# Attention ahead of two mixtures of experts: the products of a pack with v as one step, and the last 64 rows of q and k turned as whole blocks

## The chip, the cores and the metric

The kernel runs on one core of a Trainium2 chip. The metric is the device time of one execution in microseconds, lower is better. The engines are named as in the profile: PE is TensorE (PEld its weight load), DVE is VectorE, ACT is ScalarE, POOL is GpSimd, and SP is the queue that issues most transfers.

## What is computed

```python
# attention: batch 2, 8 heads, 576 rows, width 64; blocks of 64 rows
scores = q @ k.T / sqrt(64)
scores = where(row // 64 >= column // 64, scores, -1e9)
attn   = softmax(scores)                     # row maximum subtracted, 1e-9 in the sum
x      = attn @ v  ->  (1152, 512)
# layer 1: each row goes to the expert of its largest logit (8 experts, 512 -> 1024 -> 512)
x = gate * sigmoid(x @ w_output_gate)[expert] * (relu(x @ w1[expert]) @ w2[expert])
# layer 2: the same without the output gate, and with a capacity per expert
```

All data are float32. The scores and the layers are computed as three products of split halves each (a high part, a low part, and the two cross products), the products with v as plain float32.

## The kernel before, in words

The change lies in the attention, which takes the first third of the run. The two batches of a head lie side by side: tiles `qn`, `kn`, `vn` (`nat` in the code) hold 128 rows by 64 + 64 columns, in five column groups. Four are full blocks of 128 rows; the fifth holds the last 64 rows of the sequence in partitions 0 to 63. q and k are rotated over two such tiles, v over three. Partitions 64 to 127 of the fifth group of v are zeroed once at the start (L1271), since a product reads them.

`prep_steps(h)` turns q and k of a head: four whole blocks of k, then of q (L1366), and in its third step the last 64 rows of q and of k, each as a 64x64 product (L1353). Of these it makes high and low parts with ACT and DVE, and POOL adds `kf` and `qf` out of them (L1359, L1360).

A head has nine blocks of 64 query rows; they are worked off in three packs of three blocks (`packs`). For a pack there are four kinds of work:

- `qk_steps`: for each of its three blocks, the scores on PE (L1386, or L1383 for the two shortest), the row maximum on DVE (L1387), the exponentials with their sum on ACT (L1390). Each block is a step; with each comes a call of `extra_step()`, which does one step of whatever waits in the list `extra` (the preparation of the next head; at the end the routing of the first layer, `begin_first`).
- `group_steps` (`transp`): the exponentials turned in 128x128 blocks on PE (L1413), 7 blocks in two groups for the first pack, 9 blocks in three groups for the others, and copied to `tp` by ACT (L1417), the third group by DVE (L1419).
- `pv_steps` (`pv`): the products with v (L1439), by column chunk: 3, 4 or 5 chunks for the first, second, third pack, two matmuls a chunk, one per batch, each of which fills 64 of the 128 output rows. A float32 matmul shows as two records in the trace, so a chunk has four. After the last chunk come three copies to `ot` on ACT (L1442 to L1444) and four small operations on DVE (L1445 to L1450). Each chunk is a step of its own.
- the last step of `pv`: four matmul records with `mv` that bring the result into rows and give the logits (L1453, L1454), the scaling on DVE (L1457, L1459), the sum of logits (L1461, on POOL, for the last head on DVE), and then `after_pv`: the rows of `x1` to memory, the loads of v for a later head, and, for the last head's first pack, the routing is put into `extra`.

The main loop takes one step in turn of: the scores of the pack after this one, the turning of this pack, the products with v of the pack before it. Heads 6 and 7 are interleaved by packs. `extra_step` leaves out its third and fourth call once the routing has begun. After the loop the last pack's `pv_steps` are worked off with an `extra_step` each.

The order in which this text issues the instructions is not the order on the engines. In the attention a planner simulates the engines at build time with a table of costs, and gives each engine, among the instructions that are ready in that simulation, the one that the text issues first. From the first layer on, the order is that of the text.

Of the kernel before, what the change touches and what calls it, by code (L numbers as in the profile page):

```python
# [32 lines left out]
def kernel(  # L33
# [15 lines left out]
    nc = tc.nc  # L49
    V = nc.vector  # L50
    B, H, S, D = q.shape
# [3 lines left out]
    P = 128  # L55
    BLK = 64
# [30 lines left out]
    ident = const.tile([P, P], F32, name="ident")  # L87
# [653 lines left out]
    class Moe:  # L741
# [17 lines left out]
        def load(self, s, c0=0, c1=8):  # L759
            if s not in self.at:  # L760
                self.where(s)
            e, cond = self.at[s]
            load_w(self.w1, self.w2, e, c0, c1, cond=cond)
# [477 lines left out]
    with ExitStack() as actx:  # L1241
# [7 lines left out]
        def pst():  # L1249
            return ps_t.tile([P, 512], F32, tag="t", name="pst")  # L1250
# [4 lines left out]
        NC4 = S // P  # L1255
        REM = S - NC4 * P
        NR = {"q": 2, "k": 2, "v": 3}
        nat = {nm: [ap1.tile([P, NC4 + 1, 2 * D], F32, name=f"{nm}n{i}") for i in range(n)] for nm, n in NR.items()}
# [7 lines left out]
        for i in range(2):  # L1266
            for b in range(0, NB, 2):
                if i == 0:
                    nc.gpsimd.memset(pbuf[i][b][:, (b + 1) * BLK :], 0.0)
        for t_ in nat["v"]:  # L1270
            nc.gpsimd.memset(t_[REM:P, NC4, :], 0.0)  # L1271


# [46 lines left out]
        def prep_steps(h):  # L1320

            i = h % 2
            kh = ap2.tile([P, S], F32R, tag="kh", name=f"kh{h}")
            kl = ap2.tile([P, S], F32R, tag="kl", name=f"kl{h}")
            st[h] = dict(qh=qhb[i], ql=qlb[i], kh=kh, kl=kl, p=pbuf[i],
                         mx=ap2.tile([P, NB], F32, tag="mx", name=f"mx{h}", bufs=3),
                         sm=ap2.tile([P, NB], F32, tag="sm", name=f"sm{h}", bufs=3),
                         ri=ap2.tile([P, NB], F32, tag="ri", name=f"ri{h}", bufs=3), pt={})

            mv = st[h]["mv"] = mvs[h % 3]  # L1330
            for bb, r in enumerate(halves):
                for j in (bb, 2):
                    nc.gpsimd.tensor_copy(mv[r, j, D:W], wgs[r, h, :])

            def qout(ps, b0, b1):
                src = [ps[r, :].rearrange("p (b j) -> p b j", j=BLK) for r in halves]
                for r, x in zip(halves, src):
                    if h == 0 and r is halves[1]:
                        V.tensor_scalar(qhb[i][r, b0:b1, r], x, SCALE, None, op0=ALU.mult)
                    else:  # L1340
                        nc.scalar.activation(qhb[i][r, b0:b1, r], x, AF.Copy, scale=SCALE)
                for r, x in zip(halves, src):
                    V.scalar_tensor_tensor(out=qlb[i][r, b0:b1, r], in0=x, scalar=SCALE, in1=qhb[i][r, b0:b1, r].bitcast(F32), op0=ALU.mult, op1=ALU.subtract)

            def kout(ps, a, z):
                nc.scalar.copy(kh[:, a:z], ps)
                V.tensor_tensor(kl[:, a:z], ps, kh[:, a:z].bitcast(F32), op=ALU.subtract)

            for nm in ("k", "q", "r"):
                ps = pst()  # L1350
                if nm == "r":
                    for j, x in enumerate(("q", "k")):
                        nc.tensor.transpose(ps[:, j * BLK : j * BLK + REM], nat[x][h % NR[x]][0:REM, NC4, :], ident[0:REM, 0:REM])  # L1353
                    qout(ps[:, 0:BLK], NB - 1, NB)
                    kout(ps[:, BLK : 2 * BLK], NC4 * P, S)
                    if 2:
                        qf = st[h]["qf"] = ap2.tile([P, 2, P], F32, tag="qf", name=f"qf{h}")
                        kf = st[h]["kf"] = ap2.tile([P, 2 * BLK], F32, tag="kf", name=f"kf{h}")
                        nc.gpsimd.tensor_tensor(kf, kh[:, 0 : 2 * BLK].bitcast(F32), kl[:, 0 : 2 * BLK].bitcast(F32), op=ALU.add)  # L1359
                        anchors["qf", h] = nc.gpsimd.tensor_tensor(qf, qhb[i][:, 0:2, :].bitcast(F32), qlb[i][:, 0:2, :].bitcast(F32), op=ALU.add).ins  # L1360
                    ready.add(h)
                    if h + NR["q"] < H:
                        load(h + NR["q"], "kq")
                else:
                    for c in range(NC4):
                        nc.tensor.transpose(ps[:, c * P : (c + 1) * P], nat[nm][h % NR[nm]][:, c, :], ident)  # L1366
                    if nm == "q":
                        qout(ps, 0, NB - 1)
                    else:
                        kout(ps, 0, NC4 * P)  # L1370
                yield
# [53 lines left out]
        def pv(h, pk):  # L1425

            s = st[h]
            t0 = POS[packs[pk][0][0]]
            po = pst()
            hc = slice(h * D, (h + 1) * D)  # L1430
            ts_ = slice(t0, t0 + 3)
            lo, hi = slice(0, BLK), slice(BLK, P)
            nc_ = max(c for p_, c in s["pt"] if p_ == pk) + 1
            for c in range(nc_):
                w = s["pt"][pk, c]
                n = w.shape[1]
                for bb in range(B):
                    r = slice(bb * D, (bb + 1) * D)
                    nc.tensor.matmul(po[r, 0 : n * BLK], nat["v"][h % NR["v"]][:, c, r], w[:, :, r], start=(c == 0), stop=(c == nc_ - 1))  # L1439
                if c == nc_ - 1:  # L1440
                    ot = OT.next()
                    nc.scalar.copy(ot[:, 0 : 2 * BLK], po[:, 0 : 2 * BLK])  # L1442
                    nc.scalar.copy(ot[lo, P + lo.start : P + lo.stop], po[lo, 2 * BLK : 3 * BLK])
                    anchors["ot", h, pk] = nc.scalar.copy(ot[hi, P + hi.start : P + hi.stop], po[hi, 2 * BLK : 3 * BLK]).ins  # L1444
                    V.tensor_scalar_add(s["sm"][:, ts_], s["sm"][:, ts_], 1e-9)  # L1445

                    ri, sm_ = s["ri"], s["sm"]
                    V.reciprocal(ri[:, ts_], sm_[:, ts_])
                    V.reciprocal(ri[hi, t0 : t0 + 1], sm_[lo, t0 + 1 : t0 + 2])
                    V.reciprocal(ri[lo, t0 + 1 : t0 + 2], sm_[hi, t0 : t0 + 1])  # L1450
                yield
            ps = po[:, 3 * BLK : 512]
            nc.tensor.matmul(ps[:, 0 : 2 * W], ot[:, 0:P], s["mv"][:, 0:2, :], start=True, stop=True)  # L1453
            last[0] = nc.tensor.matmul(ps[:, 2 * W : 3 * W], ot[:, P : 2 * P], s["mv"][:, 2, :], start=True, stop=True).ins  # L1454
            p3 = ps[:, 0 : 3 * W].rearrange("p (t w) -> p t w", w=W)
            rb = ri[:, ts_].unsqueeze(2)
            V.tensor_tensor(x1[:, ts_, hc], p3[:, :, 0:D], rb.to_broadcast([P, 3, D]), op=ALU.mult)  # L1457
            lg = lg1[:, ts_, :] if h == 0 else ap2.tile([P, 3, 2 * E], F32, tag="lg", name=f"lg_{h}_{pk}")
            V.tensor_tensor(lg, p3[:, :, D:W], rb.to_broadcast([P, 3, 2 * E]), op=ALU.mult)  # L1459
            if h > 0:  # L1460
                (V if h == H - 1 else nc.gpsimd).tensor_tensor(lg1[:, ts_, :], lg1[:, ts_, :], lg, op=ALU.add)  # L1461
# [83 lines left out]
        for _ in prep_steps(0):  # L1545
            pass
# [6 lines left out]
        for i, (h, pk) in enumerate(stages):  # L1553
            if (h, pk) == (2, 0):
                with tc.issue_after(anchors["qf", 1]):
                    for f in later:
                        f()
                    nc.gpsimd.tensor_copy(capf, capi[:, 0:1])
                    nc.sync.dma_start(x1d[N : N + 1, :], zrow[0:1, :])
                    nc.sync.dma_start(x2d[N : N + 1, :], zrow[0:1, :])  # L1560
            if pk == 0 and h + 1 < H and h + 1 not in st:
                extra.append(prep_steps(h + 1))
            qs_ = iter(())
            tail = False
            if i + 1 < len(stages):
                while stages[i + 1][0] not in ready and extra:
                    extra_step()
                qs_ = qk_steps(*stages[i + 1], tail)
            live = [(qs_, group_steps(h, pk), before)[i_] for i_ in (0, 1, 2)]
            while live:  # L1570
                for it in list(live):
                    try:
                        next(it)
                    except StopIteration:
                        live.remove(it)
            before = pv_steps(h, pk)
# [234 lines left out]
```

## Time and profile before

| what | value |
|---|---|
| median of 3 runs | 416.88 us (416.2 to 418.99) |
| the profiled execution, its device time | 416.57 us |
| its span, first to last instruction | 414.8 us |
| PE busy in the span | 386.4 us (93%) |
| DVE | 289.4 us (70%) |
| ACT | 254.1 us (61%) |
| POOL | 101.6 us (25%) |
| granted TensorE clock, mean | 0.976 |

The busy time of PE is an upper bound of its work: matmuls overlap, and their ends are modelled, so that a stretch can show PE busy all the time though it runs below its pace. The pace is read better from the starts of the matmuls. The attention lies in the first 139 us, the two layers behind it.

### The profile page before, as it was taken

Reading aid. Unit: us, or ns where it says so; the run is one execution under the profiler, and the core shown is the slowest. Engines: PE = TensorE matmul, PEld = TensorE weight load, DVE = VectorE, ACT = ScalarE, POOL = GpSimd, SP = SyncE. Lnnn points to the kernel's source line nnn. Section 1 sums busy time; section 2 is a strip of 40 time slices with the busy share of each in tenths; the row PEclk is TensorE's granted clock in tenths of the full one; section 3 lists DMA queues with packets and bytes.
Section 4 is the critical chain, followed back from the end, with each engine's and each line's share of the span. In section 5 each row is a group of like instructions: output and inputs, shape, how many; then the busy total and the mean of one; then the engine's idle time right before and its main releaser. Section 6 shows DMA issues by size and latency. Waiting matters only on the chain. (4 is left out here: it accounts for less than half of the span.)

```text
span 414.8 us, 7835 instructions
## 1 busy us (share of the span) xinstructions
PE 386.4 (93%) x2443; PEld 295.3 (71%) x2443; DVE 289.4 (70%) x755; ACT 254.1 (61%) x531; POOL 101.6 (25%) x211
## 2 busy tenths in 40 slices
PE   4899999999996899999999999978999999999992
PEld 3677887887775678888888866656777888856540
DVE  4577667766788697798988944679789999911010
ACT  2678778878775552877878611553679998821110
POOL 8452201212100204103212110121710287200100
PEclk9999999999997999999999999978899999999998
DMA  6649932510106802991661388360795999899890
GB/s 139 114 105 285 294 103 61 144 24 7 57 22 223 297 3 84 305 345 54 216 242 52 122 335 321 137 228 2 248 384 188 333 371 401 288 384 390 297 362 29
DMA packets 65111, 82.88 MB, mean 200 GB/s; under 512 B 34368, under 2 KB 38976, under 8 KB 65060
## 3 DMA queue, kind: packets, MB, share of 16 engines
q1 hardware_dynamic: 62180, 72.98, 52.4%
q0 software_dynamic: 2880, 9.31, 6.1%
q8 instruction: 21, 0.34, 0.3%
q14 instruction: 30, 0.25, 0.2%
HBM read 91.57 MB, written 11.80 MB: 249 GB/s over the span
## 5 line engine op out<-in xcount | busy, mean ns | idle before, releaser
L187 DVE TENSOR_TENSOR wl<-raw,wh 128x1024 fp32r<-128x1024 f32 x52 | 61.3, 1220 | 2.3 <-ACT wh L169 2.3
L169 ACT CAST wh<-raw 128x1024 fp32r<-128x1024 f32 x52 | 51.5, 1052 | 1.0 <-DMA raw<-in_moe_w_dram 0.8
L719 PE MATMUL ph<-wh,xh 128*128 128x512 f32 x120 | 50.7, 422 | 1.4 <-ACT xh L708 1.4
L719 PE MATMUL ph<-wh,xl 128*128 128x512 f32 x120 | 48.6, 405 | 0.0
L719 PE MATMUL ph<-wl,xh 128*128 128x512 f32 x120 | 48.2, 402 | 0.0
L1387 DVE TENSOR_REDUCE mx<-s 128x1 f32<-128x256 f32 (+8 forms) x72 | 34.4, 486 | 17.5 <-PE s L1386 4.6
L1390 ACT ACTIVATE p<-s,mx 128x256 f32<-128x256 f32 (+8 forms) x72 | 37.8, 527 | 10.1 <-DVE mx L1387 9.2
L1413 PE MATMUL pst<-ident,p 128*128 128x128 f32 x200 | 39.1, 291 | 0.4 <-DVE lg L1459 0.3
L187 DVE TENSOR_TENSOR wl_a<-raw,wh_a 128x1024 fp32r<-128x1024 f32 x28 | 33.2, 1220 | 0.3 <-ACT wh_a L169 0.2
L1439 PE MATMUL pst<-tp,vn 128*64 128x128 f32 (+2 forms) x384 | 32.8, 297 | 0.1
L169 ACT CAST wh_a<-raw 128x1024 fp32r<-128x1024 f32 x28 | 28.1, 1061 | 5.8 <-DMA raw<-in_moe_w_dram 5.7
L733 PE MATMUL py<-wh_a,hh 128*128 128x512 f32 x72 | 30.1, 418 | 0.0
L1413 PEld LDWEIGHTS pst<-ident,p 128*128 128x128 f32 x200 | 25.4, 150 | 6.1 <-issue 2.4
L1417 ACT COPY tp<-pst 128x384 f32<-128x384 f32 (+1 forms) x48 | 24.5, 533 | 8.2 <-PE pst L1413 7.9
L733 PE MATMUL py<-wh_a,hl 128*128 128x512 f32 x72 | 28.7, 399 | 0.6 <-DVE hl L814 0.6
L733 PE MATMUL py<-wl_a,hh 128*128 128x512 f32 x72 | 28.8, 401 | 0.0
L187 DVE TENSOR_TENSOR wl_b<-raw,wh_b 128x1024 fp32r<-128x1024 f32 x24 | 28.4, 1220 | 0.6 <-ACT wh_b L169 0.5
L1386 PE MATMUL s<-kh,qh 128*128 128x320 f32 (+3 forms) x64 | 26.0, 406 | 2.7 <-ACT p L1390 1.4
L719 PEld LDWEIGHTS ph<-wh,xh 128*128 128x128 f32 x120 | 23.2, 193 | 6.4 <-ACT xh L708 1.9
L738 POOL DMA_INDIRECT out_dram<-ys,ig x7 | 11.9, 1705 | 63.5 <-ACT ys L921 57.1
L719 PEld LDWEIGHTS ph<-wh,xl 128*128 128x128 f32 x120 | 23.1, 192 | 6.1 <-DVE xl L709 1.3
L1439 PEld LDWEIGHTS pst<-tp,vn 128*64 128x64 f32 x384 | 21.1, 142 | 8.7 <-issue 3.8
(353 smaller groups left out, 868.9 us busy)
## 6 DMA issues: line engine op xcount, KB each, us to landing
raw<-in_moe_w_dram SPq DMA_DIRECT2D x132, 512.0 KB
rx<-in_moe_w_dram SPq DMA_DIRECT2D x20, 512.0 KB
out_dram<-zrow SPq DMA_DIRECT2D x9, 256.0 KB
x2d<-zrow SPq DMA_DIRECT2D x9, 256.0 KB
kn<-in_k_dram SPq DMA_DIRECT2D x16, 128.0 KB
qn<-in_q_dram SPq DMA_DIRECT2D x16, 128.0 KB
vn<-in_v_dram SPq DMA_DIRECT2D x16, 128.0 KB
x1d<-x SPq DMA_DIRECT2D x3, 576.0 KB
```

What stands on the lines that cost most here:

```text
L169: nc.scalar.copy(whs[i], raw[:, c, :] if src is None else src)
L187: V.tensor_tensor(wls[i], raw[:, c, :] if src is None else src, whs[i].bitcast(F32), op=ALU.subtract)
L719: yield nc.tensor.matmul(out_, l[:, c * P : (c + 1) * P], r[:, cols], start=(c == 0 and j == 0), stop=(c == KD - 1 and j == 2))
L733: nc.tensor.matmul(y, l[:, cs], r[:, rs], start=(first and j == 0), stop=(last and j == 2))
L738: nc.gpsimd.indirect_dma_start(out=dest, out_offset=bass.IndirectOffsetOnAxis(ap=io.bitcast(U32), axis=0), in_=ys, in_offset=None, bounds_ ...
L1386: nc.tensor.matmul(ps[:, a:z], s[l][:, b, :], s[r][:, a - o : z - o], start=(j == 0), stop=(j == 2))
L1387: anchors["mx", h, pk] = V.tensor_reduce(out=s["mx"][:, t : t + 1], in_=ps[:, o : o + n], op=ALU.max, axis=AX.X, negate=True).ins
L1390: anchors["p", h, pk] = nc.scalar.activation(s["p"][b][:, 0:n], ps[:, o : o + n], AF.Exp, bias=s["mx"][:, t : t + 1], accum_out=s["sm"][:, ...
L1413: last[0] = nc.tensor.transpose(ps[:, j * P : (j + 1) * P], s["p"][b][:, c * P : (c + 1) * P], ident).ins
L1417: anchors["tp", h, pk] = nc.scalar.copy(fp, ps[:, 0:n]).ins
L1439: nc.tensor.matmul(po[r, 0 : n * BLK], nat["v"][h % NR["v"]][:, c, r], w[:, :, r], start=(c == 0), stop=(c == nc_ - 1))
```

## The change

Three edits. The upper halves of the fifth column group are zeroed for q and k as well as for v. The last 64 rows of q and k are then turned as whole 128x128 blocks, over rows of which the lower half is zero; of the 128 result columns the first 64 are used as before. And the `yield` in `pv` moves out of the loop over the chunks: all products of a pack with v, the copies to `ot` and the four DVE operations are one step, and the products with `mv` with what follows them are the second and last.

```diff
-        for t_ in nat["v"]:
+        for t_ in nat["q"] + nat["k"] + nat["v"]:
             nc.gpsimd.memset(t_[REM:P, NC4, :], 0.0)
...
                     for j, x in enumerate(("q", "k")):
-                        nc.tensor.transpose(ps[:, j * BLK : j * BLK + REM], nat[x][h % NR[x]][0:REM, NC4, :], ident[0:REM, 0:REM])
+                        nc.tensor.transpose(ps[:, j * P : (j + 1) * P], nat[x][h % NR[x]][:, NC4, :], ident)
                     qout(ps[:, 0:BLK], NB - 1, NB)
-                    kout(ps[:, BLK : 2 * BLK], NC4 * P, S)
+                    kout(ps[:, P : P + BLK], NC4 * P, S)
...
                     V.reciprocal(ri[hi, t0 : t0 + 1], sm_[lo, t0 + 1 : t0 + 2])
                     V.reciprocal(ri[lo, t0 + 1 : t0 + 2], sm_[hi, t0 : t0 + 1])
-                yield
+            yield
             ps = po[:, 3 * BLK : 512]
```

With the step count of `pv_steps` the calls of `extra_step` shift at the end: the routing enters `extra` in the second round of its stage instead of the fourth, so its first step is called one stage's last round earlier, and the last pack's steps give two calls instead of six.

## Rows read from the trace of the kernel before

**Rows 1.** Windows: stretch, its length, busy us (instructions) by engine, clock, DMA.
```profile
20.00:118.00 98.00, 96.64 (x807) 77.16 (x806) 69.67 (x237) 76.66 (x257) 21.91 (x105) 1.00 0.42 116
118.00:131.00 13.00, 9.34 (x85) 7.65 (x81) 12.27 (x80) 8.97 (x29) 0.29 (x1) 0.92 0.49 173
```

**Rows 2.** Waits of PE from 20 to 118 us: total, times, longest.
```profile
PE s L1383 <- ACT p L1390: 0.9, 4, 0.3
```

**Rows 3.** Timeline of PE, products with v in three runs: start, length, instruction.
```profile
98.11 0.55 PE L1439 MATMUL pst<-tp,vn 128*64 128x192 f32 x4
98.59 0.66 PE L1413 MATMUL pst<-ident,p 128*128 128x128 f32 x4
99.18 0.44 PE L1439 MATMUL pst<-tp,vn 128*64 128x128 f32 x4
99.55 0.44 PE L1413 MATMUL pst<-ident,p 128*128 128x128 f32 x2
99.92 0.66 PE L1439 MATMUL pst<-tp,vn 128*64 128x128 f32 x8
100.50 0.33 PE L1366 MATMUL pst<-ident,kn 128*128 128x128 f32 x1
```

**Rows 4.** Timeline of PE, the same sixteen records in one run.
```profile
117.48 1.20 PE L1439 MATMUL pst<-tp,vn 128*64 128x192 f32 x16
118.61 0.38 PE L1386 MATMUL s<-kh,qh 128*128 128x256 f32 x1
```

**Rows 5.** Timeline of PE, four blocks turned with no change of shape behind.
```profile
46.51 0.60 PE L1366 MATMUL pst<-ident,qn 128*128 128x128 f32 x4
46.95 0.22 PE L1383 MATMUL s<-kf,qf 128*128 128x64 f32 x1
```

**Rows 6.** Timeline of PE, the first run of products with v.
```profile
19.81 0.55 PE L1439 MATMUL pst<-tp,vn 128*64 128x192 f32 x4
```

**Rows 7.** Timeline of PE, the last rows of q and k turned.
```profile
62.52 0.60 PE L1413 MATMUL pst<-ident,p 128*128 128x128 f32 x4
63.05 0.27 PE L1353 MATMUL pst<-ident,qn 64*128 64x64 f32 x1
63.17 0.22 PE L1353 MATMUL pst<-ident,kn 64*128 64x64 f32 x1
63.32 0.38 PE L1386 MATMUL s<-kh,qh 128*128 128x256 f32 x1
63.54 0.28 PE L1386 MATMUL s<-kl,qh 128*128 128x256 f32 x1
63.66 0.28 PE L1386 MATMUL s<-kh,ql 128*128 128x256 f32 x1
```

**Rows 8.** Timeline of POOL and PE in the first 17 us.
```profile
2.84 0.49 POOL L1271 MEMSET vn<- 64x128 f32 x3
...
6.42 0.37 PE L1353 MATMUL pst<-ident,qn 64*128 64x64 f32 x1
...
7.89 0.69 PE L1386 MATMUL s<-kh,qh 128*128 128x384 f32 x1 [1.01 <-DVE qh L1339]
...
9.90 0.46 POOL L1359 TENSOR_TENSOR kf<-kh,kl 128x128 f32<-128x128 f32 x1
...
16.48 0.38 PE L1383 MATMUL s<-kf,qf 128*128 128x128 f32 x2
```

**Rows 9.** Waits of SP's queue: total, times, longest.
```profile
SPq L1464 <- DVE lg L1459: 27.5, 4, 14.6
```

**Rows 10.** Timeline, the third group of a pack turned and copied.
```profile
114.54 0.44 PE L1413 MATMUL pst<-ident,p 128*128 128x128 f32 x2
...
115.01 0.42 DVE L1419 COPY tp<-pst 128x256 f32<-128x256 f32 x1 [0.33 <-PE pst L1413]
```

**Rows 11.** Timeline of PE and one window, the end of the attention.
```profile
130.14 0.19 PE L369 MATMUL pst<-a_rag,a_ohp 128*128 128x15 bf16 x1 [2.71 <-DVE a_ohp L347]
...
138.78 0.52 PE L706 MATMUL px<-ident,xg 128*128 128x128 f32 x3 [0.68 <-DVE lg L1459]
...
130.10:135.50 5.40, 5.36 (x39) 4.20 (x41) 3.90 (x18) 1.52 (x3) 1.29 (x2) 0.50 0.32 116
```

## The prediction

> **What bounds the kernel now.** I began with the windows, to see which engine limits the stretch that the change touches. From 20 to 118 us, the body of the attention, PE shows 96.64 us busy of 98.00, DVE 69.67 and ACT 76.66 [rows 1]: 99% against 71% and 78%. The waits of PE agree: the largest entry of that stretch is 0.9 us in four waits, for exponentials [rows 2]. So an instant taken from PE's own sequence there moves everything behind it. From 118 to 131 us the picture is another: DVE 12.27 us of 13.00, PE 9.34. There the routing of the first layer runs on DVE beside the end of the attention, and what PE saves is worth little.
>
> A busy PE isn't PE at its pace, so next I read the starts of its matmuls. Four blocks turned in a row take 46.95 - 46.51 = 0.44 us to the next start, 0.11 us a block [rows 5]. The products with v have another shape, 128x64 beside 128x128, and they come in pieces. One pack's sixteen records come in three runs: 98.11 to 100.50, 2.39 us, with six turned blocks between them (0.66 us at 0.11), which leaves 1.73 us for the products [rows 3]. The same sixteen records in one run take 118.61 - 117.48 = 1.13 us [rows 4]. Two runs more cost 0.60 us, so **each change into that shape and back costs 0.30 us**. The turning of the last rows shows the same: its shape is 64x128, and around it the spacing jumps [rows 7].
>
> **The change part by part.** *Products with v as one step.* From 19.81 us [rows 6] to the run at 117.48 [rows 4] the timeline has 39 runs. They belong to 21 packs (18 of heads 0 to 5, both first packs of heads 6 and 7, the second of head 6). With one run a pack, 18 runs go: 18 x 0.30 = 5.4 us. It can't be more by this edit, short of two packs' products standing side by side; if the planner still cuts some runs it is less, and nothing if it cuts as many as now. I take all 18, since the new step puts every product ahead of the next block's scores and blocks, and the planner takes the earliest of what is ready. Runs behind 118 us I count at nothing: DVE covers them [rows 1]; if it didn't, one run more (0.30) would be won.
>
> *Last rows as whole blocks.* By the starts, four blocks from 62.52 would hand over at 62.96, and the second score product starts at 63.54: 0.58 us for two turnings and one score product [rows 7]. Undisturbed that is 2 x 0.11 [rows 5] + 0.12 (63.54 to 63.66) = 0.34. Saved: 0.24 us a head. For head 0 it is nothing, as PE then waits 1.01 us for DVE anyway [rows 8]. 7 x 0.24 = 1.7 us. Whole blocks have twice the columns; what they cost in width shows in the rows, 0.12 us from the 64-column block to the next (63.05 to 63.17) against 0.11 for a whole one: no cost. Here a rule speaks against the edit: the Trainium skill (TensorE: Matmul & The Clock Gate, Back-to-back issue gap) gives about 60 cycles for up to 64 columns and 134 for 128; by it a whole block would cost an estimated 31 ns more, 16 of them 0.5 us, and the sum below would be 5.1 instead of 5.6. The trace disagrees, and the trace decides.
>
> *Zeroing.* Three memsets of this form take 0.49 us together on POOL [rows 8]; four more take 0.65 us, and end near 4.0 us. The first reader, the turning at 6.42, has 2.4 us to spare. POOL's later work slides by 0.65: `kf` from 9.90 to 10.6; its reader on PE starts at 16.48 [rows 8]. Cost nothing. Without that cover it would be 0.65. Should the loads of the last rows be made to wait for the zeroing, though they write other partitions, SP's queue would slide by about 1 us at the start; I take 0 and keep 1.0 for the range.
>
> *What moves with it.* The copies to `ot` on ACT and four small operations on DVE now stand behind the one run, ahead of the next block's maximum and exponential; the amount is the same. PE meets the products with `mv` one round later than those copies and has scores and turned blocks between. The last step of a pack moves to the second round: POOL's sum of logits, the loads of v, and the rows of `x1` on SP. SP waits up to 14.6 us for these rows, and loads of later heads queue behind them [rows 9]; their earlier place shortens that wait and frees `tp` and the PSUM tile sooner. I count it at nothing; the bounds are 0 and a gain that PE's small waits limit to 1.36 us (98.00 - 96.64).
>
> *A new wait.* In one run, PE stands in order until the last group's copy is there, and the scores of the next block queue behind it. The nearest rows: the third group's blocks start at 114.54, DVE's copy starts at 115.01 and lasts 0.42, to 115.43: 0.89 us [rows 10]. Between them and the products now lie a block of scores and a group of turned blocks: three products of 0.12 us or more and three or four blocks of 0.11, so 0.7 us or more [rows 5, 7]. So the cover is about as long as the wait. Bounds: 0, and 16 packs with a third group x 0.2 = 3.2 us. I take 1.5, near the idle 1.36 us that PE already has here.
>
> **Sum:** -5.4 - 1.7 + 1.5 = -5.6 us. The profiled execution took 416.57, which gives 411.0; the median of the runs is 0.3 above it, so I forecast **411.3** for the median. ACT would then be busy 76.66 of about 92 us, 83%, and DVE 75%: no new bound. The layers behind run on the rows that the attention hands over, so the gain carries through.
>
> **The rivals.** *The planner cuts the runs as before.* It works by readiness in its simulation, and nothing in the rows says that it knows the 0.30 us. Runs then stay near 39, and only the last rows are won: 416.9 - 1.7 = 415.2. Against it: the sixteen records of [rows 4] stand in one run though the text cuts them into four steps, so the planner joins what is ready. Chance 0.17.
>
> *Slower: the run waits for DVE's copy.* If the copy of the third group stands behind a row maximum and the four small operations, as these now come earlier, it is late by an estimated 0.7 us each time (the copy itself takes 0.42 [rows 10]; five operations, one of them wider, take more), in 16 packs 11 us, less the 7.1 saved: 416.9 + 4 = 421. It decides from 7.1 / 16 = 0.44 us a pack. For it: DVE is at 94% behind 118 us [rows 1]. Against it: it is at 71% in the body, and copies are not among PE's larger waits. Chance 0.08.
>
> *The end goes another way.* The routing's first step is called one round earlier. PE now waits 2.71 us for the one-hot rows at 130.14; behind that wait the granted clock is 0.50, the 1.2 GHz level, for 5.4 us [rows 11], which costs half of them, 2.7. The first layer starts at 138.78, held by the attention's last logits. If the routing's products stand earlier on PE than the last packs' work, that wait grows and the last logits come later: some 4 us of the gain go, 415.3, chance 0.10. If DVE's chain comes sooner and PE meets it ready, wait and low clock shrink and up to 3 to 4 us more are won: 408, chance 0.12.
>
> **How the numbers follow.** Forecast 0.53, planner 0.17, new wait 0.08, end longer 0.10, end shorter 0.12. About 1% (4.2 us) is what a measurement here can tell from none: faster means under 412.7. The forecast's own band, from its bounds, runs from 409.5 (no new wait) to 413.5 (3.2 us of it and a few cut runs); 0.47 of its 0.53 lie under 412.7. With the shorter end, faster is 0.59. Slower is the new wait, 0.08. The rest, 0.33, is within 1%. The range reaches from 407.5 (shorter end) to 416.5 (planner, longer end); outside lie the new wait and the odd mishap, under 2 in 10.
>
> **What would show it.** Right: in the timeline the products with v stand in about one run a pack, x12, x16, x20; the last rows' blocks follow each other at 0.11 us with no jump around them; the run that stood at 117.48 starts near 112; the first layer's blocks start near 133 instead of 138.78. Wrong: as many runs as now; PE waits for `tp` from DVE summing to several us; the wait for the one-hot rows far from 2.71 us, with more or less of the stretch at clock 0.50; or a later layer that loses what the attention won, as waits for weights.

## The result, and the profile after

The changed kernel is slower. Its median is 423.28 us (422.96 to 425.26, 4 runs) against 417.77 us for the kernel before in the same comparison (416.2 to 418.99, 4 runs): a ratio of 1.0139, interval 1.0103 to 1.0176. The forecast was 411.3, the range ended at 416.5. The profiled execution took 423.02 us with a span of 421.3, which is 6.5 more than before's 414.8.

The first view is the windows of the kernel after, over the first stretch of [rows 1] (length, then busy us and instructions of PE, PEld, DVE, ACT and POOL, clock, DMA), with the stretch ahead of 97 us, in which the waits of DVE below are counted:

```profile
20.00:97.00 77.00, 72.17 (x631) 61.61 (x629) 56.05 (x190) 61.68 (x203) 19.54 (x98) 0.99 0.50 140
20.00:118.00 98.00, 91.58 (x790) 77.87 (x787) 69.44 (x234) 76.55 (x252) 21.89 (x104) 0.98 0.41 116
```

In the body PE has gone from 96.64 us busy [rows 1] to 91.58, so it is idle 6.42 us instead of 1.36; and fewer of its instructions are through by 118 us (790 against 807). As the timelines below show, PE gets through a piece of work sooner and then waits. The waits of PE, from 20 to 118 us, after (total, times, longest), to be read against the one entry of [rows 2]:

```profile
PE s L1386 <- ACT p L1390: 2.1, 4, 1.3
PE pst L1413 <- ACT tp L1417: 1.9, 3, 0.6
PE s L1383 <- ACT p L1390: 1.6, 5, 0.4
```

All three are waits for ACT. None is for DVE's copy of a third group. The longest, 1.30 us, stands alone, at 110.23. Where do the others stand? The timeline of PE after, from the products with v of one pack to those of the next (start, length, instruction; in brackets the idle time ahead of it and what ended that):

```profile
59.65 1.22 PE L1439 MATMUL pst<-tp,vn 128*64 128x192 f32 x20
60.80 0.66 PE L1366 MATMUL pst<-ident,qn 128*128 128x128 f32 x4
...
61.91 0.60 PE L1413 MATMUL pst<-ident,p 128*128 128x128 f32 x4
62.34 0.27 PE L1353 MATMUL pst<-ident,qn 128*128 128x128 f32 x1
62.45 0.27 PE L1353 MATMUL pst<-ident,kn 128*128 128x128 f32 x1
62.48 0.36 PE L1386 MATMUL s<-kh,qh 128*128 128x256 f32 x1
62.68 0.28 PE L1386 MATMUL s<-kl,qh 128*128 128x256 f32 x1
...
63.19 0.34 PE L1454 MATMUL pst<-mv,ot 128*128 128x80 f32 x2
64.16 0.33 PE L1413 MATMUL pst<-ident,p 128*128 128x128 f32 x1 [0.63 <-ACT tp L1417]
64.88 0.43 PE L1383 MATMUL s<-kf,qf 128*128 128x64 f32 x2 [0.39 <-ACT p L1390]
...
65.72 0.36 PE L1386 MATMUL s<-kh,qh 128*128 128x192 f32 x1 [0.28 <-ACT p L1390]
...
66.22 0.98 PE L1439 MATMUL pst<-tp,vn 128*64 128x192 f32 x12
...
92.78 0.34 PE L1454 MATMUL pst<-mv,ot 128*128 128x80 f32 x2
...
110.23 0.47 PE L1386 MATMUL s<-kh,qh 128*128 128x448 f32 x1 [1.30 <-ACT p L1390]
```

The same place in the timeline of PE before, with its counterpart two heads later:

```profile
59.91 0.55 PE L1439 MATMUL pst<-tp,vn 128*64 128x192 f32 x4
...
60.98 0.89 PE L1439 MATMUL pst<-tp,vn 128*64 128x192 f32 x16
61.80 0.47 PE L1386 MATMUL s<-kh,qh 128*128 128x448 f32 x1
...
64.11 0.34 PE L1454 MATMUL pst<-mv,ot 128*128 128x80 f32 x2
...
64.49 0.98 PE L1439 MATMUL pst<-tp,vn 128*64 128x192 f32 x12
65.43 0.43 PE L1383 MATMUL s<-kf,qf 128*128 128x64 f32 x2
...
93.38 0.34 PE L1454 MATMUL pst<-mv,ot 128*128 128x80 f32 x2
```

The first part of what was forecast is there: the twenty records stand in one run from 59.65 and hand over at 60.80, where before they came in two pieces and were through only at 61.80. So the products with `mv` start 64.11 - 63.19 = 0.92 us earlier. Then PE stands still for 0.63, 0.39 and 0.28 us, 1.30 in all. Before, the next pack's twelve products with v stood at that place, 64.49 to 65.43, and filled it; now they come at 66.22, behind scores that wait for ACT. From one such place to the next, two heads later, before needs 93.38 - 64.11 = 29.27 us and after 92.78 - 63.19 = 29.59. **What the shapes saved, the waits took back.** The same three waits with the same lengths stand at 93.76, 94.48 and 95.31.

Behind these the loss is more than their length. The windows of the kernel after around that place:

```profile
92.00:94.00 2.00, 1.37 (x11) 1.11 (x9) 1.60 (x4) 1.96 (x5) 0.78 (x4) 1.00 0.40 91
94.00:96.00 2.00, 1.33 (x9) 0.95 (x10) 1.57 (x7) 1.75 (x8) 0.97 (x2) 1.00 0.00 0
96.00:98.00 2.00, 2.00 (x15) 1.53 (x14) 1.77 (x10) 1.08 (x6) 0.00 (x0) 0.50 0.00 0
98.00:100.00 2.00, 2.00 (x12) 1.93 (x11) 0.38 (x2) 1.06 (x3) 0.00 (x0) 0.65 0.00 0
```

PE is busy 1.37 and 1.33 us of two times 2.00, and the granted clock then falls to 0.50, the 1.2 GHz level, and is back only within the fourth window. Before shows 1.00 in all four. The loss is an estimated 2.00 x 0.50 + 2.00 x 0.35 = 1.7 us.

The end adds its own. The rows that answer to [rows 11], from the timeline of the kernel after, with the first gather of rows for the first layer (POOL) and one window, then before's first gather:

```profile
134.19 0.18 PE L369 MATMUL pst<-a_rag,a_ohp 128*128 128x15 bf16 x1 [0.86 <-DVE a_ohp L347]
...
136.92 1.17 POOL L205 DMA_INDIRECT xg<-x1d,a_ids  x1 [5.60 <-DVE a_iof L387]
...
142.11 0.63 PE L706 MATMUL px<-ident,xg 128*128 128x128 f32 x4 [1.44 <-DMA xg<-x1d,a_ids]
...
144.00:146.00 2.00, 2.00 (x5) 1.49 (x5) 1.90 (x6) 0.25 (x1) 0.00 (x0) 0.50 0.96 348
```

```profile
133.91 1.17 POOL L205 DMA_INDIRECT xg<-x1d,a_ids  x1 [12.53 <-DVE a_er L379]
```

The gather starts 136.92 - 133.91 = 3.0 us later. The first layer starts at 142.11 instead of 138.78, now held by its gathered rows, and a further stretch at 0.50 follows it. Taken together: +2.6 us at the products with `mv` of head 7's first pack (119.7 against 117.1), +3.3 at the first layer's start, +4.7 behind the stretch at 144 to 147, +6.5 at the end. So most of the 3.3 is the body's. What makes the last 1.8, behind 148 us, stays open.

### The profile page after: what moved, and what is told of

The parts are those of the page before. It is cut to its first block, busy times and chain, and to the rows that moved or that the text cites. A ratio compares the mean times of both kernels' runs of the same rounds, so it can differ in the third digit from the quotient of the medians.

```text
span 421.3 us, 7842 instructions
## 1 busy us (share of the span) xinstructions
PE 386.2 (92%) x2443; PEld 300.8 (71%) x2443; DVE 290.2 (69%) x755; ACT 256.1 (61%) x531; POOL 104.0 (25%) x215
## 5 line engine op out<-in xcount | busy, mean ns | idle before, releaser
L1387 DVE TENSOR_REDUCE mx<-s 128x1 f32<-128x384 f32 (+8 forms) x72 | 34.8, 488 | 29.5 <-PE s L1386 21.1
L1390 ACT ACTIVATE p<-s,mx 128x384 f32<-128x384 f32 (+8 forms) x72 | 37.9, 528 | 14.6 <-DVE mx L1387 14.0
L1386 PE MATMUL s<-kh,qh 128*128 128x320 f32 (+4 forms) x64 | 26.5, 414 | 4.5 <-ACT p L1390 3.2
L1439 PE MATMUL pst<-tp,vn 128*64 128x128 f32 (+2 forms) x384 | 29.9, 296 | 0.4 <-DVE kl L1347 0.3
L1439 PEld LDWEIGHTS pst<-tp,vn 128*64 128x64 f32 x384 | 22.5, 142 | 6.5 <-issue 2.0
L719 PEld LDWEIGHTS ph<-wl,xh 128*128 128x128 f32 x120 | 23.5, 196 | 4.7 <-DVE wl L187 0.6
```

Of the source, the lines that this page charges most:

```text
L719: yield nc.tensor.matmul(out_, l[:, c * P : (c + 1) * P], r[:, cols], start=(c == 0 and j == 0), stop=(c == KD - 1 and j == 2))
L1386: nc.tensor.matmul(ps[:, a:z], s[l][:, b, :], s[r][:, a - o : z - o], start=(j == 0), stop=(j == 2))
L1387: anchors["mx", h, pk] = V.tensor_reduce(out=s["mx"][:, t : t + 1], in_=ps[:, o : o + n], op=ALU.max, axis=AX.X, negate=True).ins
L1390: anchors["p", h, pk] = nc.scalar.activation(s["p"][b][:, 0:n], ps[:, o : o + n], AF.Exp, bias=s["mx"][:, t : t + 1], accum_out=s["sm"][:, ...
```

## The experiments

Each edit is a few lines. The two parts of the change were first run alone, then the step was moved. The rows of each run are those of one profiled execution.

**One step alone** (`e1_steps`): last rows turned as before, without the four memsets.

```diff
-        for t_ in nat["q"] + nat["k"] + nat["v"]:
+        for t_ in nat["v"]:
...
-                        nc.tensor.transpose(ps[:, j * P : (j + 1) * P], nat[x][h % NR[x]][:, NC4, :], ident)
+                        nc.tensor.transpose(ps[:, j * BLK : j * BLK + REM], nat[x][h % NR[x]][0:REM, NC4, :], ident[0:REM, 0:REM])
...
-                    kout(ps[:, P : P + BLK], NC4 * P, S)
+                    kout(ps[:, BLK : 2 * BLK], NC4 * P, S)
```

> Only the products with v as one step; the last rows turned as before. The order on PE is that of the changed kernel. Theory A: this edit brings the new waits, so it is as slow as the changed kernel or, with the 0.24 us a head not saved, up to 1.7 us slower: 5.5 to 7.5 us over before; the three waits that repeat every two heads (1.3 us of gaps) are there. Rival (the whole blocks of q and k do the harm): within 1 us of before, or faster.

Measured: 425.4 us, ratio 1.0135 (1.0068 to 1.0202), the changed kernel's 1.0139. The loss belongs to the one step. (Where ratios are given, they are against the kernel before in the same comparison.)

**Whole blocks alone** (`e2_rows`): the changed kernel with the `yield` of the products back inside the loop over groups, as before.

```diff
-            yield
+                yield
             ps = po[:, 3 * BLK : 512]
```

> Only the last rows of q and k turned as whole blocks; the products with v keep their steps. The order of the instructions on PE is that of the kernel before, so this prices the edit by itself. Theory A (the saving at changes of shape is real, and the changed kernel loses it again in waits of PE and at the end of the attention): the six warm heads each save 0.24 us by the starts, and where PE waits for ACT soon after, less; 1.0 to 1.7 us faster than before. Rival (a turned block over 128 rows costs more, or the zeroing delays the start): as slow as before or up to 1 us slower.

Measured: 421.36 us, ratio 1.0014 (0.9969 to 1.006). No gain of 1.7 us; the rival had the time right. Why is seen at the place of [rows 7], in the timeline of this kernel, PE first, then ACT:

```profile
62.47 0.60 PE L1413 MATMUL pst<-ident,p 128*128 128x128 f32 x4
62.90 0.27 PE L1353 MATMUL pst<-ident,qn 128*128 128x128 f32 x1
63.01 0.27 PE L1353 MATMUL pst<-ident,kn 128*128 128x128 f32 x1
63.19 0.39 PE L1386 MATMUL s<-kh,qh 128*128 128x256 f32 x1
63.42 0.28 PE L1386 MATMUL s<-kl,qh 128*128 128x256 f32 x1
...
63.68 0.54 PE L1453 MATMUL pst<-mv,ot 128*128 128x160 f32 x2
...
62.31 0.74 ACT L1390 ACTIVATE p<-s,mx 128x576 f32<-128x576 f32 x1
...
63.42 0.21 ACT L1444 COPY ot<-pst 64x64 f32<-64x64 f32 x1
```

The two blocks do follow at 0.11 us. But the next score product starts 0.18 us behind the second block, at 63.19, after ACT's exponential (62.31 + 0.74 = 63.05); in the changed kernel, where the exponential is long done, it starts 0.03 us behind it (62.45 to 62.48). The products with `mv` start at 63.68, after ACT's last copy to `ot` (63.42 + 0.21 = 63.63); before they started at 63.78. So from the four blocks to the second score product it is 63.42 - 62.47 = 0.95 us, against 1.02 in [rows 7] and 62.68 - 61.91 = 0.77 in the changed kernel. By these times the next instruction waited most of the gain away. No idle time is shown for it: the modelled end of the second block, 63.01 + 0.27 = 63.28, reaches beyond the next start.

**All rounds, routing in its place** (`e3_rounds`): the step keeps the place of the products but gives back the rounds that were removed, so that the routing is called as before.

```diff
-            yield
+            for _ in range(nc_):
+                yield
             ps = po[:, 3 * BLK : 512]
```

> The changed kernel, but after the one step with all products of a pack come as many empty steps as before, so that the products with mv, what hangs on them and the calls of the routing stand in the same rounds as in the kernel before. In the body the order on PE is that of the changed kernel; it differs behind about 117 us. Theory A (two losses, body and end): the body stays as in the changed kernel, its first pack of head 7 some 2.6 us behind the kernel before, the end is as before; 2 to 3.5 us over before. Rival B (the loss is the earlier routing alone): the body's lag is made up and the kernel is 3 us or more faster than before. Rival C (empty steps change nothing): 5.5 us over before.

Measured: 425.81 us, ratio 1.013 (1.0065 to 1.0195): the time of rival C, not of theory A. PE waits for ACT from 20 to 97 us for 1.9, 1.2 and 0.6 us in the same three kinds (the changed kernel: 1.9, 1.6 and 0.8), and behind these waits the clock falls here too, but at other places:

```profile
38.00:40.00 2.00, 2.00 (x13) 1.67 (x10) 0.82 (x6) 0.78 (x4) 0.00 (x0) 0.50 1.01 383
```

So it does from 68 to 70 us, and not behind the third of the places; in `e1_steps` likewise. What such a stretch costs can be read from the starts: the run of twenty stands at 61.33 and, two heads later, at 92.49, in the changed kernel at 59.65 and 89.24. That is 1.68 us behind one stretch and 3.25 behind two.

That the routing is called earlier is not the cause of the body's loss: at head 7's first pack this kernel is later still (122.5 against before's 117.1), and the first product of the routing on PE stands only behind it (126.5). Nor did the end come out as before, as theory A had it: PE waits 4.45 us for the one-hot rows (2.71), the first gather starts at 139.14 (133.91), the first layer at 145.51 (138.78).

**The step in the last round** (`e4_late`): all products of the pack stand where the last group's step stood.

```diff
             nc_ = max(c for p_, c in s["pt"] if p_ == pk) + 1
+            for _ in range(nc_ - 1):
+                yield
             for c in range(nc_):
```

> The changed kernel, but the empty steps come first, so that all products of a pack stand in one step in the place of its last chunk, and the rest as in the kernel before. By the order on PE 23 runs. Theory A (the losses come from where the planner puts the copies to ot and the scores around an early run, not from the one run itself): the waits that repeat every two heads are gone or other, the 0.30 us a run and 0.24 us a head are won, 3 to 7 us faster than before. Rival C (one long run starves ACT and DVE, and PE waits afterwards wherever it stands): waits of PE of 5 us or more between 20 and 118 us, no faster than before.

Measured: 413.37 us, ratio 0.9869 (0.9808 to 0.993). The same single step, put later, is faster than both kernels, as theory A had it.

**The step in the second round** (`e5_second`): one `yield` at that place.

> Edit: the changed kernel with one yield ahead of the loop over the groups of the products with v, so the one step stands in the second round of a block instead of the first; last rows as whole blocks. By the kernel's order 24 runs of products with v, as few as in the changed kernel (24) and the late form (23, ratio 0.987). Theory (the place of the step decides: the earlier the run stands on PE, the longer DVE and ACT lack scores, and the longer PE waits for them later): between the early form (1.014) and the late one (0.987), nearer the late one since the next block's scores and its turned q now stand ahead of the run: 0.99 to 1.003, DVE's maximum waits for scores for less than 13 us in 20 to 97 us. Rival one (any single run, wherever it stands, costs the waits; the late form won by its end alone, the gathers 8 us earlier): 1.01 or more, with the milestones of the body late as in the changed kernel. Rival two (only a run in the very first round hurts): 0.987, as the late form.

Measured: 412.25 us, ratio 0.9854 (0.9775 to 0.9933). I had put it between the early and the late form; it equals the late one, so rival two was right on this: of the three places, only the very first round hurts. Its timeline of PE, from the run of twenty on, and the window of the body:

```profile
58.77 1.22 PE L1440 MATMUL pst<-tp,vn 128*64 128x192 f32 x20
...
62.08 0.35 PE L1455 MATMUL pst<-mv,ot 128*128 128x80 f32 x2
62.62 0.36 PE L1386 MATMUL s<-kh,qh 128*128 128x192 f32 x1 [0.19 <-ACT p L1390]
...
63.76 0.98 PE L1440 MATMUL pst<-tp,vn 128*64 128x192 f32 x12
...
89.64 0.34 PE L1455 MATMUL pst<-mv,ot 128*128 128x80 f32 x2
...
20.00:97.00 77.00, 75.33 (x686) 65.63 (x684) 58.11 (x198) 64.27 (x219) 20.29 (x101) 1.00 0.50 140
```

Behind the products with `mv` PE waits 0.19 us instead of 1.30, and the twelve products of the next pack follow at 63.76 instead of 66.22. Two heads take 89.64 - 62.08 = 27.56 us against before's 29.27. In the same 77 us PE hands out 686 instructions against 631 in the changed kernel, ACT is busy 64.27 us against 61.68, and the clock stays at 1.00. What DVE waited for tells of the supply. The largest entry of its waits from 20 to 97 us, in the changed kernel, then in this one:

```profile
DVE mx L1387 <- PE s L1386: 13.8, 14, 1.8
```

```profile
DVE mx L1387 <- PE s L1386: 5.6, 11, 0.8
```

So with the step in the first round DVE lacks scores for 13.8 us, its maxima come later, ACT's exponentials behind them, and PE meets ACT unready; with the step one round later the scores stand ahead. That chain is read from the order and these sums. The entry alone doesn't rank kernels: before shows only 1.7 us of it and is slower than this form.

**The late form with the old rows** (`e6_late_rows`): the late form with the edit of `e1_steps`.

> Edit: the late form (all products with v in the place of the last group's step) with the last rows of q and k turned as before, 64 partitions into 64 columns, and without the four added memsets. PE's order is that of the late form; only the price of the turning differs, and this time with ACT less loaded between the blocks. Theory (alone the edit of the rows gave nothing, ratio 1.001, because the score product behind the rows waited for ACT's exponential; with the step late the same wait is still there): within 1 us of the late form, so 0.985 to 0.992. Rival (the price of 0.24 us a head as forecast, uncovered now that PE leads): 1.7 us slower than the late form, about 0.991. The two overlap in the time; the milestones by 117 us tell them apart: within 0.3 us of the late form, or 1.4 to 1.7 us behind it.

Measured: 417.06 us, ratio 0.9966 (0.9929 to 1.0002), some 3.7 us above the late form: the time missed both expectations. The milestone speaks against the rival: at head 7's first pack it stands at 111.3 us, the late form at 111.6. The difference arises behind, at the first layer. The windows of this kernel, where the late form shows 1.00 in both:

```profile
138.00:140.00 2.00, 2.00 (x6) 1.59 (x5) 1.66 (x6) 0.26 (x1) 0.00 (x0) 0.50 0.01 2
140.00:142.00 2.00, 2.00 (x12) 1.58 (x12) 0.00 (x0) 0.31 (x1) 0.00 (x0) 0.74 0.00 0
```

Of the 2.5 us between the two spans (414.2 and 411.7), this stretch at the lower level is 2.00 x 0.50 + 2.00 x 0.26 = 1.5. Whether the old rows bring it on, or it comes and goes with small shifts of the order, is the question of the next run.

**The second-round form with the old rows** (`e8_second_rows`), to see whether that was the rows' doing:

> Edit: the second-round form (ratio 0.985) with the last rows of q and k turned as before, and without the four added memsets; the order on PE is otherwise that of the second-round form. It asks whether the whole blocks are worth anything once the step stands well, or whether the 3.7 us between the late form (413.4) and the late form with the rows as before (417.1) arose behind the attention. In those two the milestones of the body agree within 0.7 us (the one with the old rows even ahead), and the difference appears at 136 to 148 us, where one shows a granted clock of 0.50 and the other 1.00. Theory (the whole blocks give nothing; where the low clock falls at the first layer is set by waits of another origin): milestones by 117 us within 0.7 us of the second-round form; the time within 1.5 us of it if the stretch at 0.50 falls alike, 411 to 414, and any larger difference lies behind 125 us and shows in the clock. Rival (the whole blocks are worth 0.24 us a head on a path that now binds): 1.4 us behind by 117 us, 414 to 416.

Measured: 413.32 us, ratio 0.9847 (0.9791 to 0.9902), the second-round form's 0.9854. Its run of twenty stands at 59.73 and two heads later at 87.30, 27.57 us; the second-round form's at 58.77 and 86.32, 27.55. The whole blocks are worth nothing in the body. By the starts they do save 0.10 us behind the run of twenty (58.77 to the second score product at 60.31, 1.54 us, against 59.73 to 61.37, 1.64), but then PE waits 0.16 us for ACT at 61.09, a wait that the old rows don't have; the products with `mv` stand 3.31 us behind the run's start in both. This kernel stands 1.0 us later all through the body, more than the 0.7 of the theory, but it does so from its first pack on. PE's first block waits for the load of k until 4.49 us here and until 4.17 there. In the late pair it is the other way about: the old rows start at 4.18, the whole blocks at 4.57, and the old rows are ahead by 0.7 us at the first pack. So the start goes with that load and not with the rows. A stretch at 0.50 falls at its first layer too (136 to 138 us), where the second-round form shows none, and the median is 1.1 us higher, which the intervals don't tell from none. So the price in the body is settled; why the late form loses 3.7 us with the old rows stays open, beyond the 1.5 us that the clock shows.

**The routing one call later** (`e7_late_route`), on the late form, where PE waits 4.99 us for the rag rows:

```diff
-                if calls[0] in (3, 4):
+                if calls[0] in (3, 4, 6):
```

> Edit: the late form with the routing of the first layer let through at one call less (one number added to a tuple), so that its products with the rag rows stand one call later on PE, behind a run of products with v, nine turned blocks and another such run. In the late form PE waits 4.99 us for DVE's rag rows at 125.05 and then shows a granted clock of 0.50 from 120 to 129. Theory (PE's order put those products too early for DVE; work that is ready stands behind them): the wait shrinks by the work moved ahead of it, some 2 to 3 us, and the low clock with it; 1 to 4 us faster than the late form, ratio 0.977 to 0.985. Rival (the gather of the first layer's rows hangs on that chain, and comes later by as much): no gain, or 1 us slower, 0.987 to 0.990, with a longer wait for the gathered rows at the first layer.

Measured: 420.47 us, ratio 1.0033 (1.0001 to 1.0065), 7 us slower than the late form. The rival was right in kind and far too small. The timeline of this kernel, and then of the late form, both with POOL's first gather:

```profile
131.67 1.17 POOL L205 DMA_INDIRECT xg<-x1d,a_ids  x1 [0.64 <-DVE a_pi L275]
...
138.04 1.09 PE L706 MATMUL px<-ident,xg 128*128 128x128 f32 x4 [5.27 <-DMA xg<-x1d,a_ids]
```

```profile
125.05 0.25 PE L369 MATMUL pst<-a_rag,a_ohp 128*128 128x15 bf16 x3 [4.99 <-DVE a_rag L362]
...
125.86 1.17 POOL L205 DMA_INDIRECT xg<-x1d,a_ids  x1 [5.42 <-DVE a_er L379]
...
135.02 0.63 PE L706 MATMUL px<-ident,xg 128*128 128x128 f32 x4 [0.68 <-PE pst L1456]
```

The wait of 4.99 us went, and a wait of 5.27 us for the gathered rows came at the first layer, with the granted clock at 0.50 from 136 to 145 us, the first two of them while PE still waits. In the late form the gather starts 131.67 - 125.86 = 5.8 us earlier, beside attention work that PE still has. A stalled PE there was the cheaper of the two.

## Why the prediction was wrong

**The sizes that were read off PE's shapes held.** The 39 runs of products with v, of 21 packs, became 24 in the changed kernel (23 of them ahead of 118 us, the last pack's at 124.82); 18 fewer were forecast, 15 were had, 15 x 0.30 = 4.5 us. The second-round form has 21, all 18 fewer. The price comes out where little takes it back: in two heads before has 11 runs and the second-round form 6, and it needs 29.27 - 27.56 = 1.71 us less, 0.34 for each of the five, if all of it is put down to the runs. At head 7's first pack that form is 5.0 us ahead of before (112.1 against 117.1), where 5.4 was forecast for the shapes. The whole blocks follow at 0.11 us, also as forecast, and their 0.24 us is there by the starts: with the step in the same place, the stretch from the four blocks to the second score product takes 0.77 us with them and 64.86 - 63.84 = 1.02 with the old rows (`e1_steps`). That is so in every second head; in the others it is some 0.14.

**The step that failed is "What moves with it".** I wrote that the copies to `ot` and the small operations now stand ahead of the next block's maximum and exponential, "the amount is the same", and counted the new order at nothing. The amount is the same, and the order was the price. Behind it stands the reading that an instant taken from PE's sequence "moves everything behind it": I had read 99% busy as PE bounds, ACT at 78% follows. But before's PE had no wait there because its pieces of products with v stood where ACT was late (64.49 to 65.43). Put into one step in the first round, they no longer stand there, and DVE gets its scores later. A rough bill for the body of the profiled execution: -4.5 for the shapes, +5.1 of idle time (6.42 - 1.36), +1.7 for the stretch at 0.50, makes +2.3; measured +2.6 at head 7's first pack. Of the other 3.9 us, 0.7 come up by the first layer's start, where the gather is late, 1.4 at one more stretch at the lower level, and 1.8 behind it.

That the place is the cause is shown, by one and the same step in three places (1.0139, 0.9854, 0.9869). That it acts by the pieces as filling, and not by some other consequence of the order, is read from the timelines and was not tried apart from it: the order on PE, DVE and ACT moves together.

**"Last rows as whole blocks" failed the same way.** The price was right at the place where it was read; that it moves what stands behind was not. In `e2_rows` the score product and the products with `mv` behind the blocks wait most of it away, in the second-round form the next score product does (0.10 us saved, 0.16 waited), and neither kernel gains time by it. The rule weighed there, about 60 cycles for 64 columns and 134 for 128 (the Trainium skill, TensorE: Matmul & The Clock Gate, Back-to-back issue gap), is not what decided: the two whole blocks follow each other at 0.11 us (62.34 to 62.45) as the narrow ones did at 0.12.

**"A new wait"** was looked for at the wrong engine. No wait of PE for a copy of a third group by DVE shows in the body; it waits for ACT, 5.6 us in the three entries above, where 1.5 was taken and 3.2 was the bound. The "slower" rival came near the time (421) by the same wrong engine, which is luck. It had 0.08.

**"The end goes another way"** was half right. The routing's place does move several us (`e7_late_route`), but by these runs the lever is when the gather starts, not how long PE waits for the one-hot rows: in the changed kernel that wait fell from 2.71 to 0.86 us and the first layer came later all the same.

## What to carry to other kernels

An engine that is 99% busy may owe that to small ready pieces that fill its waits for the next engine: before joining pieces into one block, look at what stands behind each of them and ask what the engine will do there without it. If a block pays by itself, try it in several places of the order before judging it; here one `yield` was worth some 3% (1.0139 against 0.9854). And a stall is not a cost by itself: ask what the instruction behind it starts, as the gather here, before moving it away.

## What the hardware showed that I had not expected

- Short waits can cost twice. After 1.30 us of waits within 2.2 us (93.1 to 95.3) the granted clock stood at 0.50 from 96 us and was back within 98 to 100; the loss of 1.7 us is more than the waits. The same three waits around 35 and 65 us had no such consequence in this execution, nor had the one wait of 1.30 us ahead of 110.23: there the clock reads 1.00 throughout. In `e1_steps` and `e3_rounds` it fell behind the first two of the places and not behind the third. No kernel here without such waits shows the lower level between 20 and 118 us. So what a wait costs by the clock could not be forecast from its length alone.
- A change of TensorE's shape, from 128x128 to 128x64 and back, costs 0.30 us by the spacing, and some 0.34 by the time of two heads with five runs fewer. The Trainium skill (TensorEngine Tiling (Array Packing), Key Properties) says that changing the mode drains the engine; the wider spacing agrees and gives the price, while no row shows the draining itself.
- A short wait of PE need not appear as idle time, since the shown ends of matmuls reach beyond the next start (0.27 us shown, 0.11 us to the next). The sign of it is a spacing wider than the same product has elsewhere: 0.18 us behind the second block in `e2_rows`, 0.03 in the changed kernel.
